# A head loop with memory features: five loads three steps later, and one constant on another engine

## Chip, cores and metric

The kernel runs on one core of a Trainium2 chip. The metric is the time of one execution on the device, in microseconds. Of the kernel before there are three timed runs: 708.89, 709.9 and 713.49 us, median 709.9. One execution was profiled; it took 710.93 us, and the span from its first to its last instruction is 709.2 us.

## What is computed

Two independent parts are computed and set side by side. Part B is a two-dimensional spectral filter (a real FFT over 2048 x 576, a product with learned weights, the inverse). Part A is attention with a compressive memory: 32 heads of width 18, and a sequence of 2048 rows in four segments of 512. In each segment a head attends within the segment, and also reads from a memory that was filled by the segments before. The change is in part A. The reference, cut to it:

```python
phi = lambda t: jnp.where(t > 0, t + 1.0, jnp.exp(t))
for s in range(N):                       # N = 4 segments of L = 512
    qs, ks, vs = q[:, :, s], k[:, :, s], v[:, :, s]
    p = _softmax(jnp.einsum("bhqd,bhkd->bhqk", qs, ks) * scale + mask, axis=-1)
    a_dot = jnp.einsum("bhqk,bhkd->bhqd", p, vs)
    pq = phi(qs)
    num = jnp.einsum("bhld,bhde->bhle", pq, M)
    den = jnp.einsum("bhld,bhd->bhl", pq, z)[..., None] + 1e-6
    o = g * (num / den) + (1.0 - g) * a_dot
    M = M + jnp.einsum("bhld,bhle->bhde", phi(ks), vs)
    z = z + jnp.einsum("bhld->bhd", phi(ks))
```

The features pq are phi(q). Segment 0 (the first) finds an empty memory and needs none; the second segment, g=1 in the code, is the first to read them. The 1e-6 is the small constant of the denominator's reciprocal.

## The kernel before

The kernel has three stages. In the first the forward FFT runs while part A's weights are split. In the second, the projections of part A are computed; queries, keys, values and the features go to DRAM, the queries and keys as three bf16 pieces each, whose sum has the precision of float32. The inverse FFT follows. The third stage is the attention; it holds the change.

**The head loop.** `attention` (L928) is a loop over t=0 to 132, one step per head and segment. Steps come in blocks of eight heads, a stack n = t//8; a segment is four stacks, 32 steps. Each step issues work of several pipeline depths at once:

- `s1` (L637) for head t+10: three score matmuls (L652 with L653, then two at L644) in PSUM banks of a tag with three buffers, and on VectorE the row maxima of them (L654, L648). It is the first work of a step.
- `s2` (L680) for head t: scores again (L688, L692, L693, L697), now transposed and with the maxima folded in; ScalarE takes the exponentials (L689, L694, L698). Every fourth step GpSimd then masks four blocks (L701).
- `pv` (L709): the product with the values, on alternate steps from t=5; `pv_out` (L721) copies the result to U, and `u_dmas` (L725) sends a stack's sums (rD, one transfer) and rows (uD, four) to DRAM.
- `mpath` (L662): every fourth step the maxima are split by GpSimd (L669, L670), turned by TensorE (L674) and written as two further rows of the query stack by a DMA that GpSimd issues (L678).

**The order of work** is written out by hand: each engine takes its instructions in program order, and SyncE issues nearly all DMAs in program order as well. At the first step of a stack (t%8 = 0) a list q is filled: six transfers of query stack n+2 (`stack_dmas`, tile Qs, three buffers), six of key stack n+3 (tile Ks; one of the four key buffers and one of the three query buffers are called x in the profile), and one `load_v` (tile vs). Each of the six moves 18 partitions of 8 heads, 144 KB. Two entries of the list are issued per step, so the queries go in steps t%8 = 0 to 2, the keys in 3 to 5, vs in 6. The sums and rows of an earlier stack (rD, uD) are interleaved with them in steps t%8 = 4 to 6. SyncE's DMAs use eight completion semaphores in turn; an issue waits until the DMA that used the same one before, eight issues earlier, has landed.

The query stack loaded in steps 16 to 18 (stack 4) takes the buffer of stack 1, which s2 reads until step 15. Because `s1` runs ten steps ahead, it is first read in step 22, by `s1` of head 32. The next one (stack 5) is loaded from step 24 on and first read in step 30.

**The features.** `pq_load` (L759, the DMA at L763) loads one of five tiles of features (126 partitions x 512 float32, the last 72 partitions) into one of five buffers. For the second segment it is called in the head loop, once a step, ahead of the step's entries of the list. In later segments `mem1` reloads a buffer when it has been read. The readers are `den` (L765), a generator put into the background list at t=34, whose matmuls (L772) form the denominators, and `mem1` (L788).

**The reciprocals.** `recip` (L736) is a generator that moves on once a step. It loads a 128 x 128 tile `ry` of denominators (L739), waits three steps, adds the constant if asked (L743), takes the reciprocal on VectorE (L744), scales it on ScalarE (L746), splits it into three bf16 pieces (L747 to L750, ScalarE and GpSimd) and sends these to DRAM. It runs eight times in all. Three of them, one for each of the segments 1 to 3, are called by `den` with the constant (`eps` true); the other five divide by the softmax sums and have none.

Of the kernel before, what the change touches and what calls it, by code (L numbers as in the profile page):

```python
# [389 lines left out]
class ATT:  # L390
# [345 lines left out]
    def recip(s,src,dst,gate,eps,load,slack=0):  # L736
        nc=s.nc; tp=s.tp
        w=tp.tile([128,3,128],BF,name="rw",bufs=2); y=tp.tile([128,128],F32,name="ry",bufs=2)
        nc.sync.dma_start(y,src.rearrange("h (b c) -> (h b) c",b=4))  # L739
        yield  # L740
        yield
        yield
        if eps: nc.vector.tensor_scalar(y,y,1e-6,None,op0=OP.add)  # L743
        nc.vector.reciprocal(y,y)  # L744
        yield
        nc.scalar.activation(y,y,AF.Copy,scale=gate)  # L746
        nc.scalar.copy(w[:,0],y)  # L747
        nc.gpsimd.tensor_tensor(y,y,w[:,0],op=OP.subtract)
        nc.gpsimd.tensor_copy(w[:,1],y)
        nc.gpsimd.tensor_tensor(w[:,2],y,w[:,1],op=OP.subtract)  # L750
        for _ in range(slack): yield
        nc.sync.dma_start(bass.AP(tensor=dst.tensor,offset=dst.offset,ap=[[128,128],[32*512,3],[1,128]]),w)
        yield
        yield
        r=tp.tile([96,512],BF,name=load,bufs=1) if load!="re" else tp.tile([126,1024],BF,name="re",tag="pq",bufs=5)[:96,:512]
        nc.sync.dma_start(r,dst)
        s.rc[load]=r
        yield
# [169 lines left out]
    def attention(s,tp,ps):  # L928
        nc=s.nc; s.tp,s.ps,s.psm,s.mtag=tp,ps,s.ps1,"s1"
        s.homes()  # L930
        def steps(gen,i):
            for _ in range(i):
                try: next(gen)
                except StopIteration: return
# [5 lines left out]
        def run_bg(rate):  # L940
            state["acc"]+=rate
            if state["acc"]>=1:
                state["acc"]-=1
                while bg:
                    try: next(bg[0]); break
                    except StopIteration: bg.pop(0)
        lane=[]
        s.cap=tp.tile([128,128],F32,name="cap",bufs=1)
        for t in range(133):
            k,hh=divmod(t,4); n,qd=divmod(k,2); g=k//8  # L950
            if t==3: nc.gpsimd.memset(s.cap,3.0e38)
            if t==4: nc.gpsimd.affine_select(out=s.cap,in_=s.cap,pattern=[[1,128]],compare_op=OP.is_ge,fill=0.0,base=0,channel_multiplier=-1)
            if hh==0 and qd==0:
                if 0<n<14: q+=s.stack_dmas(n+2,0)
                if 0<n<13: q+=s.stack_dmas(n+3,1)
                if n+2<16: q.append(lambda n=n: s.load_v(n+2))
            st=t%32
            if 16<=t<21: s.pq_load(1,t-16)
            if t==34: bg.append(s.den(1,lane))
            if st==8 and g>0:  # L960
                def ln(g=g):
                    r=s.recip(s.rD[g-1],s.rrD[g-1],s.g1,False,"rr",2)
                    for i in range(8):
                        next(r)
                        if 2<i<6: s.ux_load(g-1,i-3)
                        yield
                    yield from r
                    bg.append(s.mixed(g))
                    if g<3: bg.append(s.den(g+1,lane))
                    if g<3: bg.append(s.oproj(g-1))  # L970
                lane.append(ln())
            if t==124: lane.append(s.recip(s.rD[3],s.rrD[3],s.g1,False,"rr"))
            if 125<=t<128: s.ux_load(3,t-125)
            a=s.s1(t+10) if t+10<128 else iter(())
            b=s.s2(t) if t<128 else iter(())
            if q: q.pop(0)()
            if qu: qu.pop(0)()
            if hh==3 and m is not None: steps(m,1)
            steps(a,1)
            steps(b,1)  # L980
            r=(t-5)%4
            if r%2: run_bg(1)
            steps(a,1)
            steps(b,1)
            if 5<=t<129: s.pv((t-5)//4,(t-5)%4)
            if t==129:
                for j in range(4): s.pv(31,j)
                s.pv_out(31)
                u=s.u_dmas(15)
                rb=s.recip(s.rD[3],s.rrD[0],s.g1,False,"re")  # L990
                qu+=[u[0],lambda: next(rb)]+u[1:]
            steps(a,1)
            steps(b,1)
            if hh==2 and m is not None: steps(m,1)
            if hh==1 and k+2<32: m=s.mpath(k+2); next(m)
            if 7<=t<131 and t%4==3:
                s.pv_out((t-7)//4)
                if t%8==3:
                    u=s.u_dmas((t-11)//8)
                    if t<120: s.later(1,lambda u=u: qu.extend(u))  # L1000
                    else: qu+=u
            for l in list(lane):
                try: next(l)
                except StopIteration: lane.remove(l)
            if q: q.pop(0)()
            if qu: qu.pop(0)()
            run_bg((.3,1,.5,1)[r])
            s.due(t)
# [30 lines left out]
        nc=s.nc  # L1039
# [108 lines left out]
```

## Time and profile before

| What | Value |
|---|---|
| three timed runs | 708.89, 709.9, 713.49 us |
| median | 709.9 us |
| profiled execution | 710.93 us |
| its span | 709.2 us |
| TensorE matmul busy | 676.4 us (95%) |
| VectorE busy | 556.2 us (78%) |
| ScalarE busy | 441.0 us (62%) |
| GpSimd busy | 208.8 us (29%) |
| chain that ended last | TensorE 61%, VectorE 9%, DMA 6%, ScalarE 5% |
| moved by DMA | 121.04 MB, mean 171 GB/s |

In the profile PE is TensorE, PEld its weight loads, DVE VectorE, ACT ScalarE, POOL GpSimd and SPq SyncE's issue of DMAs. A row of the timeline has its start in us, its duration, engine, line of the kernel, operation, output<-inputs, and in brackets the idle time of the engine before it with what ended it. Releasers are inferred from semaphores, and several transfers share one, so the name in brackets can be that of a neighbour. A row of the table of windows has the stretch, its length, the busy time of each engine with its count of instructions, the granted share of TensorE's clock, the mean busy share of the core's 16 DMA engines, and GB/s. TensorE is busy in nearly all of the span; its idle places and its granted clock say where time can be won or lost.

### The profile page before, as it was taken

The page shows a single profiled execution, that of the slowest core. Times are in us where ns is not written, and L with a number is a line of the kernel's source. Part 1 is how long each engine was busy: PE and PEld are TensorE (multiplying, and loading weights), DVE is VectorE, ACT ScalarE, POOL GpSimd, SP SyncE. Part 2 cuts the span into 40 slices and gives each one's busy share as a digit, 9 for nine tenths or more (in the row PEclk, how much of TensorE's full clock was granted, in tenths as well). Part 3 has the DMA queues.
Part 4 walks back from the last instruction along what each step waited for, and adds up shares of the span by engine and source line. Part 5 has one row for each costly group of instructions (what it writes and reads, how often), then busy time and mean ns, then how long its engine had stood idle before and what let it go on. Part 6 is the DMA issues. An engine that isn't in the chain of part 4 may idle for free.

```text
span 709.2 us, 14168 instructions
## 1 busy us (share of the span) xinstructions
PE 676.4 (95%) x4861; PEld 498.7 (70%) x4861; DVE 556.2 (78%) x1233; ACT 441.0 (62%) x994; POOL 208.8 (29%) x409
## 2 busy tenths in 40 slices
PE   4999999999999999999999899999999999998997
PEld 4999779889879888999844444444566445764677
DVE  6999999899989889887588688877666876568153
ACT  3657695574574563444388677777666676567741
POOL 2110000100100111565165334555233753246210
PEclk9999999999999999999999999999999999999999
DMA  9876546555563568899647666676556765441331
GB/s 343 272 233 205 150 141 194 175 178 167 165 211 133 165 215 279 201 239 211 180 109 176 172 161 154 173 181 169 128 129 185 171 164 128 122 129 52 99 100 69
DMA packets 83388, 121.04 MB, mean 171 GB/s; under 512 B 11368, under 2 KB 50902, under 8 KB 83180
## 3 DMA queue, kind: packets, MB, share of 16 engines
q1 hardware_dynamic: 76724, 104.11, 51.8%
q0 software_dynamic: 6592, 16.03, 8.2%
q8 instruction: 38, 0.62, 0.4%
q14 instruction: 34, 0.28, 0.1%
HBM read 81.78 MB, written 38.24 MB: 169 GB/s over the span
## 4 chain that ended last, share of the span: by engine, by line
PE 61%; DVE 9%; DMA 6%; ACT 5%; issue 3%; POOL 3%; DVEq 0%; SPq 0%; ACTq 0%; POOLq 0%
PE pv L718 9%; PE po L861 7%; PE pj L464 6%; PE pjv L464 6%; PE s L644 5%; PE i L300 4%; PE i L311 4%; PE s L652 3%; PE s L688 3%; PE po L892 2%; DVE junk L648 2%; PE s L692 2%; PE pn L791 2%; PE pm L524 2%; PE s L653 2%
## 5 line engine op out<-in xcount | busy, mean ns | idle before, releaser
L648 DVE CUSTOM_DVE_ANT_0 junk<-s,mask 128x512 bf16<-128x512 f32 (+1 forms) x256 | 141.8, 554 | 55.1 <-PE s L644 44.3
L654 DVE TENSOR_REDUCE mx<-s 128x4 f32<-128x512 f32 x128 | 87.9, 687 | 20.0 <-PE s L653 18.2
L689 ACT ACTIVATE P<-s 128x512 f32<-128x512 f32 x128 | 77.2, 603 | 24.1 <-PE s L688 20.9
L718 PE MATMUL pv<-P,vs 128*32 128x512 f32 (+3 forms) x1024 | 82.3, 440 | 0.0
L694 ACT ACTIVATE P<-s 128x512 f32<-128x512 f32 x128 | 77.1, 602 | 6.9 <-PE s L693 3.8
L698 ACT ACTIVATE P<-s 128x256 f32<-128x256 f32 x128 | 49.6, 387 | 49.7 <-PE s L697 49.6
L701 POOL TENSOR_SCALAR_AFFINE_SELECT P<-P 128x512 f32<-128x512 f32 x116 | 69.4, 635 | 5.6 <-ACT P L689 4.7
L718 PEld LDWEIGHTS pv<-P,vs 128*32 128x32 f32 x1024 | 26.9, 109 | 45.0 <-issue 42.9
L464 PE MATMUL pj<-x,wqkh 128*128 128x512 f32 x162 | 56.1, 407 | 0.0
L210 DVE TENSOR_TENSOR t<-Z 128x580 f32<-128x580 f32 x64 | 46.7, 757 | 0.2
L514 POOL MEMSET vt<- 128x32 f32 x16 | 2.4, 159 | 148.8 <-PE pm L524 121.5
L210 DVE TENSOR_TENSOR Z<-t 128x580 f32<-128x580 f32 x64 | 45.9, 756 | 0.0
L644 PE MATMUL s<-Ks,Qs 108*128 108x512 bf16 (+1 forms) x128 | 42.2, 330 | 0.0
L488 ACT CAST sp<-pj 128x512 bf16<-128x512 f32 x36 | 21.1, 585 | 30.7 <-DVE pj L484 30.7
L142 PE MATMUL f<-ftab,eh 128*128 128x290 f32 (+1 forms) x160 | 31.6, 317 | 9.0 <-DMA ftab<-ftab 9.0
L300 PE MATMUL i<-civ,Y 128*128 128x256 f32 (+1 forms) x288 | 37.9, 284 | 1.6 <-DVE T L332 1.6
L300 PEld LDWEIGHTS i<-civ,Y 128*128 128x128 f32 (+1 forms) x288 | 35.8, 181 | 1.8 <-DVE T L332 1.8
L311 PE MATMUL i<-itab,T 128*128 128x290 f32 (+1 forms) x224 | 36.4, 312 | 0.0
L464 PEld LDWEIGHTS pj<-x,wqkh 128*128 128x128 f32 x162 | 30.4, 188 | 8.4 <-issue 1.7
L669 POOL CAST mh<-mg 128x16 bf16<-128x16 f32 x32 | 6.8, 214 | 99.1 <-ACT mg L667 67.9
L464 PE MATMUL pj<-xh,wqkh 128*128 128x512 f32 x90 | 35.6, 395 | 0.0
L464 PE MATMUL pj<-xh,wqkl 128*128 128x512 f32 x90 | 35.6, 395 | 0.0
(214 smaller groups left out, 1859.6 us busy)
## 6 DMA issues: line engine op xcount, KB each, us to landing
qkD<-sp SPq DMA_DIRECT2D x36, 384.0 KB
Ks<-qkD SPq DMA_DIRECT2D x72, 144.0 KB
x<-qkD SPq DMA_DIRECT2D x60, 144.0 KB
Qs<-qkD SPq DMA_DIRECT2D x60, 144.0 KB
xin<-xb SPq DMA_DIRECT2D x16, 384.0 KB
cfw<-cfw POOLq DMA_DIRECT2D x16, 384.0 KB, 4.5
civ<-civ POOLq DMA_DIRECT2D x16, 384.0 KB, 7.5
vs<-vD SPq DMA_DIRECT2D x16, 330.0 KB
```

Of the source, the lines that this page charges most:

```text
L210: v.tensor_tensor(o,a,b,op=op)
L300: nc.tensor.matmul(p[:m,k],Y[i][:,q,c*128:c*128+m],cc[:,hl,o:o+256],start=n==0,stop=n==5)
L311: nc.tensor.matmul(p,x,t,start=n==0,stop=n==6)
L464: s.nc.tensor.matmul(out,a,b,start=i==0,stop=i==len(L)-1)
L644: nc.tensor.matmul(out,Q[:108,h,128*i:128*i+128],K[:108,h,:128*(i+1)],start=True,stop=True)
L648: nc.vector.tensor_tensor_reduce(out=junk[:,:w],in0=src,in1=s.mask[:,512-w:],scale=1.0,scalar=-3.0e38, op0=OP.add,op1=OP.max,accum_out=s.m ...
L654: nc.vector.tensor_reduce(out=s.mx[k][:,hh],in_=pa.rearrange("p (b c) -> p b c",c=128),axis=mybir.AxisListType.X,op=OP.max)
L689: nc.scalar.activation(P[0][:,hh],p0,AF.Exp,scale=SC)
L694: nc.scalar.activation(P[1][:,hh],p1,AF.Exp,scale=SC)
L701: if k<29: nc.gpsimd.affine_select(out=x,in_=x,pattern=pat+[[1,128]],compare_op=OP.is_ge,fill=0.0,base=0,channel_multiplier=-1)
L718: nc.tensor.matmul(s.pvt[32*hh:32*hh+32,128*j:],vt[:,j,19*h:19*h+32],mv[0][:,hh,mv[1]],start=j==0,stop=j==2,skip_group_check=True)
L861: nc.tensor.matmul(ps,a[t][:r,c],b[:r,t,w],start=i==0,stop=i==14)
```

## The change

Two lines change. The five feature loads of the second segment are issued at t=19 to 23 instead of t=16 to 20; within the step the call stands where it stood, ahead of the step's list entries. The order on SyncE's queue was pq, two Qs, pq, two Qs, pq, two Qs, pq, two Ks, pq, Ks, rD, Ks, uD and so on; it becomes six Qs, pq, two Ks, pq, Ks, rD, Ks, uD, pq, Ks, uD, Ks, uD, pq, vs, uD, pq. And the addition of the constant in `recip` is issued on GpSimd; the reciprocal that follows stays on VectorE.

```diff
-        if eps: nc.vector.tensor_scalar(y,y,1e-6,None,op0=OP.add)
+        if eps: nc.gpsimd.tensor_scalar(y,y,1e-6,None,op0=OP.add)
...
-            if 16<=t<21: s.pq_load(1,t-16)
+            if 19<=t<24: s.pq_load(1,t-19)
```

## Prediction

> **What bounds the kernel now.** I read the page, then the chain of waits, then the waits and the timeline of TensorE around the moved loads (steps t=16 to t=32 of the head loop), then SyncE's own queue there, and last the table of windows for the clock and the DMA share. The chain is 61% TensorE, and in the attention part TensorE runs on almost without a break, so time is worth something only where it stops. In order, the rows below are one line of the chain and six of TensorE's timeline. The L697 matmul is the last of a step and L652 the first of the next.
>
> ```profile
> 390.54 6.15 DMA Ks<-qkD
> ```
> ```profile
> 390.63 0.27 PE L697 MATMUL s<-Qs,Ks 110*128 110x256 bf16 x1
> ...
> 394.50 0.28 PE L697 MATMUL s<-Qs,Ks 110*128 110x256 bf16 x1
> 396.82 0.38 PE L652 MATMUL s<-x,Qs 108*128 108x384 bf16 x2 [2.06 <-DMA Ks<-qkD]
> ...
> 402.11 0.28 PE L697 MATMUL s<-Qs,Ks 110*128 110x256 bf16 x1
> ...
> 413.77 0.28 PE L697 MATMUL s<-x,Ks 110*128 110x256 bf16 x1
> 413.88 0.38 PE L652 MATMUL s<-Ks,Qs 108*128 108x384 bf16 x2
> ```
>
> At step t=22 (s1(32), the first use of query stack 4) TensorE stands 2.06 us for a DMA: the only wait of TensorE for a transfer in the whole attention part. Two steps without a stop take 3.87 us (390.63 to 394.50); the two with it take 7.61 (394.50 to 402.11). So this place costs 3.74 us: 2.06 idle, and about 1.7 more. The other 1.7 is the granted clock in the table of windows (columns: PE, PEld, DVE, ACT, POOL busy, PEclk, DMA share, GB/s):
>
> ```profile
> 366.00:372.00 6.00, 6.00 (x51) 3.25 (x52) 5.18 (x16) 5.37 (x13) 4.14 (x7) 1.00 0.63 147
> ...
> 396.00:402.00 6.00, 5.17 (x34) 2.41 (x34) 3.12 (x8) 2.77 (x6) 1.98 (x4) 0.72 0.62 175
> ...
> 408.00:414.00 6.00, 6.00 (x57) 2.88 (x56) 5.04 (x16) 4.43 (x11) 3.00 (x5) 1.00 0.65 145
> ...
> 420.00:426.00 6.00, 6.00 (x47) 2.23 (x46) 4.10 (x14) 4.35 (x12) 0.42 (x2) 1.00 0.62 159
> ...
> 428.00:432.00 4.00, 4.00 (x37) 2.06 (x35) 3.51 (x13) 3.25 (x8) 1.28 (x3) 1.00 0.40 105
> ```
>
> In 396 to 402 the clock is 0.72: 6 x 0.28 = 1.7 us lost after the stop. The last-but-one column matters as much. Whatever is going on, the DMA share lies at 0.62 to 0.65 in these windows and falls to 0.40 only after 428. I read the flat 0.62 as the ceiling of these transfers: a stack transfer fills 18 partitions a piece and does not spread over all 16 engines, and the ones that it uses are never free.
>
> By the Trainium skill, "DMA: Bandwidth & Descriptors", section "Why a DMA increments its semaphore by 16 and not by 1", a SyncE transfer runs on the largest number of engines up to 16 that divides its slowest dimensions. Eighteen rows give nine engines, a share of 9/16 = 0.56. The plateau agrees, the other transfers making up the rest.
>
> SyncE's queue shows how the transfers stand in line:
>
> ```profile
> 381.98 0.32 SPq L763 DMA_DIRECT2D pq<-pqD  x1
> ...
> 386.65 0.32 SPq L763 DMA_DIRECT2D pq<-pqD  x1
> 387.02 1.25 SPq L628 DMA_DIRECT2D Qs<-qkD  x2
> 388.82 0.32 SPq L763 DMA_DIRECT2D pq<-pqD  x1
> 390.54 1.12 SPq L628 DMA_DIRECT2D Ks<-qkD  x2
> 392.53 0.30 SPq L763 DMA_DIRECT2D pq<-pqD  x1
> 393.43 0.27 SPq L628 DMA_DIRECT2D Ks<-qkD  x1
> 394.80 0.55 SPq L729 DMA_DIRECT2D rD<-U  x1
> 395.39 0.45 SPq L628 DMA_DIRECT2D Ks<-qkD  x1
> 396.54 0.27 SPq L734 DMA_DIRECT2D uD<-U  x1
> ...
> 402.56 3.73 SPq L628 DMA_DIRECT2D Qs<-qkD  x6
> 407.29 1.53 SPq L628 DMA_DIRECT2D Ks<-qkD  x3
> 411.11 0.54 SPq L729 DMA_DIRECT2D rD<-U  x1
> 411.70 0.46 SPq L628 DMA_DIRECT2D Ks<-qkD  x1
> 412.20 0.35 SPq L734 DMA_DIRECT2D uD<-U  x1
> 412.59 0.32 SPq L628 DMA_DIRECT2D Ks<-qkD  x1
> 413.43 0.27 SPq L734 DMA_DIRECT2D uD<-U  x1
> ```
>
> An issue takes over the semaphore of the one eight before it, and waits until that one has landed. So the eighth issue after a transfer tells when it was down. The sixth piece of query stack 4 (the second of the two at 387.02) has uD at 396.54 as its eighth: it landed at 396.5, and TensorE starts 0.28 later. The "Ks" that the wait row and the chain name is not wanted until t=30; the queries are what was missing. The sixth piece of stack 5 (end of the group at 402.56) has uD at 413.43 as its eighth. Its first use, L652 of t=30, begins at 413.88, right behind L697, with no idle. That is 0.45 us after the landing, of which 0.28 is the way from landing to start. Stack 5 comes 0.17 us before it would stop TensorE as well.
>
> **The loads, moved.** Five pq transfers (L763) go from t=16 to 20 to t=19 to 23, on SyncE's queue alone; nothing is added, and the issues (0.32 us each) are the same five. Between them they pass the six Qs pieces, the six Ks pieces, rD, the four uD and one vs. Three of them (381.98 to 386.65) stood in front of the last Qs piece, and no longer do.
>
> *At t=22.* Between the two landings (396.54 and 413.43, 16.89 us) lie twenty transfers: two pq, six Ks, six Qs, one rD, four uD, one vs. That is 0.84 us each. Three fewer in front bring stack 4 in 2.5 us earlier, at 394.0. By bytes it is more: 3 x 126 x 512 x 4 bytes at the 175 GB/s of the window is 4.4 us, which gives 392.1. TensorE is ready at 394.78 (end of L697). Both ends are early enough, so the stop goes: -3.74 us, clock included.
>
> *At t=30.* This is what is late next. Stack 5 cannot overtake: ahead of it in the line, before and after the change, stand the same five pq, six Qs, six Ks, rD, four uD and vs. The order among them is all that differs. If the engines that carry them were never free before, the last piece of stack 5 lands at 413.43 again. TensorE however comes 3.74 us earlier, at 413.88 - 3.74 = 410.14. It then waits until 413.43 + 0.28 = 413.71: +3.57 us. Bounds: 0, if there were gaps to fill; +3.57 if there were none. I take +3.57, as the plateau shows no gap and eight transfers are always open.
>
> *The clock after it.* The stop of 2.06 us cost 1.7 behind it; a stop of 1.58 elsewhere cost nothing:
>
> ```profile
> 282.15 2.04 PE L300 MATMUL i<-civ,Y 128*128 128x256 f32 x15 [1.58 <-DVE T L332]
> ```
> ```profile
> 282.00:284.00 2.00, 1.85 (x15) 1.85 (x16) 0.53 (x2) 0.12 (x1) 1.06 (x3) 1.00 0.93 197
> ```
>
> So the bounds for a stop of 3.57 are 0 and +1.7, and the nearer row is that of 2.06: I take +1.7. Before, those 1.7 us lay ahead of t=30 and were covered, because the queries of t=30 would not have been there sooner. Now they come behind t=30, where nothing waits, and are paid in full. The stage from t=32 on has room: the DMA share falls to 0.40 in it.
>
> By the Trainium skill, "TensorE: Matmul & The Clock Gate", section "Why this matters for your kernels", idle gaps over about 3 us between matmuls bring the half clock. The trace differs: 2.06 us was enough here. By that rule a stop of 3.57 still pays the 1.7, and the sum stays; were the stop under 3, it would be 0 and the sum +1.4 - 1.7 = -0.3, the second rival below.
>
> *Who reads pq.* The first reader is den(1):
>
> ```profile
> L772 PE MATMUL pd<-pq,zst x30: 592/605/617, 422.3 to 593.6; 126*32 126x512 f32 x24, 72*32 72x512 f32 x6
> ```
>
> It starts at 422.3. All pq are in line before stack 5, so down by 413.4: 8.9 us of cover. Nothing.
>
> **The constant on GpSimd.** Three times L743 leaves VectorE (0.22 us) and becomes a GpSimd instruction on which VectorE's reciprocal, next in VectorE's order, waits. Below are the group of the nearest GpSimd operation on this tile and rows of the three places.
>
> ```profile
> L748 POOL TENSOR_TENSOR ry<-ry,rw x8: 426/427/431, 446.1 to 683.1; 128x128 f32<-128x128 f32 x8
> ```
> ```profile
> 440.94 0.22 POOL L670 TENSOR_TENSOR mh<-mg,mh 128x16 bf16<-128x16 f32 x1
> 442.26 0.22 DVE L743 TENSOR_SCALAR ry<-ry 128x128 f32<-128x128 f32 x1
> 446.65 0.38 PE L652 MATMUL s<-Ks,x 108*128 108x384 bf16 x2 [0.93 <-DVE mx L654]
> ```
> ```profile
> 525.98 0.95 DVE L744 RECIPROCAL ry<-ry 128x128 f32<-128x128 f32 x1
> 526.28 0.22 POOL L670 TENSOR_TENSOR mh<-mg,mh 128x16 bf16<-128x16 f32 x1
> ```
> ```profile
> 616.34 0.22 POOL L670 TENSOR_TENSOR mh<-mg,mh 128x16 bf16<-128x16 f32 x1
> 619.74 0.22 DVE L743 TENSOR_SCALAR ry<-ry 128x128 f32<-128x128 f32 x1
> ```
>
> Its duration is bounded by 0.22 (the VectorE row) and 0.43 (L748, two inputs, same shape); I take 0.35 as one input on GpSimd lies between. In the first place GpSimd is free from 441.16, done by 441.6, and VectorE saves 0.25 at 442.26; VectorE is what TensorE waits for there (0.93 at 446.65), so up to -0.25. In the third GpSimd is free from 616.56, three microseconds ahead: VectorE saves 0.25, TensorE does not wait for it: 0. In the second GpSimd comes to it only after L670, at 526.5; the reciprocal starts at about 527.0 instead of 525.98. That is 1.0 us of VectorE, of which TensorE sees what three score banks do not absorb: between 0 and +1.0. The next score into that bank is due at 528.6 and its reduction would end about then, so I take +0.15. What GpSimd does next (a query DMA, then masks) waits for other engines in every place and starts no later. Sum: -0.1, bounds -0.5 and +1.0.
>
> **Sum.** -3.74 + 3.57 + 1.7 - 0.1 = +1.4 us. The profiled execution took 710.93 us (span 709.2), 1.0 over the median of 709.9, which itself has 708.89 to 713.49 around it. On the profiled one it gives 712.3; on the median 711.3, which I predict. About 1% (7.1 us) is what a measurement of this kernel can tell from no change.
>
> **The rivals.**
> First, the stop goes and does not come back. This needs free engine time between 382 and 413, about 3.6 us of it in 31. A share of 0.62 speaks for it if it is read as room; the steady plateau, the eight open transfers and the landing only 0.17 us ahead of t=30 speak against it. -3.74 - 0.1: 706.1.
> Second, the stop moves to t=30 but the clock stays up, or drops where TensorE has slack: -3.74 + 3.57 - 0.1 = -0.3, so 709.6. The 1.58 us stop speaks for it, the 2.06 us one against. This is also the case in which the change does nothing.
> Third, slower: the stop at t=30 brings two half-clock stretches. One place, one mechanism: if a stop of about 2.06 fills enough of one clock interval, one of 4.12 can spoil two. It decides from an idle of 4.12 on, thus if stack 5 lands 0.55 us later than I have it. Price +0.55 + 1.7 over the sum: +3.65, 713.6.
>
> **How the numbers follow.** Chances: my forecast 0.55, the second rival 0.2, the first 0.15, the third or a worse second place on GpSimd 0.10. The forecast's own range is 710.4 to 712.9, from the bounds of the constant (+1.1, -0.4) and half a microsecond either way for the two landings. With the second rival this holds 0.75, so the range reaches to the first too: 706.0 to 713.2. All cases lie within 1% of 709.9 (702.8 to 717.0): within 1% 0.94, faster by over 1% 0.02, slower by over 1% 0.04 for what a second late stack would add.
>
> **What would show it.** Right: no wait of TensorE at t=22; one of 3 to 4 us on L652 at t=30, with six Qs pieces landing at about the same time after t=16 as before; clock 1.00 around t=23 and a dip in the 6 us behind t=30; TensorE waiting for no DMA after that. The reciprocal of the second place starts some 0.5 us behind L670. Wrong: no wait at t=30 (then the engines had room); a share well over 0.65 in the stretch; or VectorE standing more than a microsecond for GpSimd in any place.

## Result and profile after

| What | Before | Changed |
|---|---|---|
| median | 710.6 us (20 runs, 707.47 to 713.49) | 715.08 us (20 runs, 711.32 to 718.65) |
| ratio of the times | | 1.0069, 95% interval 1.0053 to 1.0085 |
| profiled execution (span) | 710.93 us (709.2) | 711.75 us (710.0) |
| mean granted clock of the runs | 0.9979 to 0.9986 (three groups of runs beside the experiments) | 0.9957 |

The change costs 4.5 us. That is within 1%, as forecast, but 3.8 us above the forecast number, and above the upper end of the range. The profiled execution of the changed kernel is one of its fastest (711.75 against a median of 715.08), so its trace shows only a small part of the loss. This governs the whole reading below.

TensorE around the moved loads, and the starts of steps t=14, 38, 70 and 78, in the changed kernel's timeline:

```profile
379.36 0.38 PE L652 MATMUL s<-Ks,x 108*128 108x384 bf16 x2
...
395.47 0.28 PE L697 MATMUL s<-Qs,Ks 110*128 110x256 bf16 x1
395.58 0.38 PE L652 MATMUL s<-x,Qs 108*128 108x384 bf16 x2
...
411.08 0.27 PE L697 MATMUL s<-x,Ks 110*128 110x256 bf16 x1
413.06 0.39 PE L652 MATMUL s<-Ks,Qs 108*128 108x384 bf16 x2 [1.71 <-DMA Qs<-qkD]
...
430.69 0.38 PE L652 MATMUL s<-Ks,x 108*128 108x384 bf16 x2
...
467.62 0.38 PE L652 MATMUL s<-x,Qs 108*128 108x384 bf16 x2 [1.42 <-DMA Ks<-qkD]
...
512.08 0.38 PE L652 MATMUL s<-Ks,Qs 108*128 108x384 bf16 x2
...
538.84 0.38 PE L652 MATMUL s<-Ks,Qs 108*128 108x384 bf16 x2
```

At t=22 (395.58) L652 follows L697 directly: the stop is gone. At t=30 (413.06) TensorE waits 1.71 us for the queries. A second stop of 1.42 us stands at t=54 (467.62), the first use of the third segment's first query stack. Its table of windows, for the stretches of before:

```profile
396.00:402.00 6.00, 6.00 (x53) 3.01 (x55) 5.35 (x19) 5.11 (x14) 3.42 (x7) 1.00 0.76 197
...
408.00:414.00 6.00, 4.29 (x37) 1.98 (x35) 3.65 (x12) 3.30 (x9) 1.34 (x4) 1.00 0.64 167
414.00:420.00 6.00, 6.00 (x54) 3.14 (x56) 5.37 (x17) 5.08 (x13) 3.00 (x5) 1.00 0.71 200
420.00:426.00 6.00, 6.00 (x53) 2.20 (x45) 4.11 (x12) 4.35 (x11) 0.99 (x3) 1.00 0.62 160
```

In this execution the clock column stays at 1.00 behind the stop. The last column but one reaches 0.76 and 0.71, so the 0.62 of before was no ceiling. The trace of before shows that as well, in windows that the prediction left out:

```profile
384.00:390.00 6.00, 5.78 (x54) 2.81 (x57) 5.47 (x18) 4.93 (x13) 1.81 (x6) 1.00 0.82 195
...
402.00:408.00 6.00, 6.00 (x54) 3.28 (x51) 5.18 (x16) 4.75 (x12) 1.53 (x4) 1.00 0.71 165
...
414.00:420.00 6.00, 6.00 (x51) 3.16 (x49) 5.36 (x17) 5.03 (x13) 3.41 (x7) 1.00 0.74 179
...
432.00:436.00 4.00, 3.63 (x33) 1.64 (x31) 3.16 (x11) 2.77 (x8) 2.12 (x5) 1.00 0.88 189
```

The second place of the reciprocals, with all engines:

```profile
525.92 0.22 POOL L670 TENSOR_TENSOR mh<-mg,mh 128x16 bf16<-128x16 f32 x1
526.23 0.53 POOL L743 TENSOR_SCALAR ry<-ry 128x128 f32<-128x128 f32 x1
526.79 0.95 DVE L744 RECIPROCAL ry<-ry 128x128 f32<-128x128 f32 x1 [1.34 <-POOL ry L743]
...
527.66 0.63 DVE L654 TENSOR_REDUCE mx<-s 128x4 f32<-128x512 f32 x1
...
528.34 0.22 PE L674 MATMUL mt<-idb,mh 128*128 128x128 bf16 x1 [1.05 <-DVE mx L654]
```

GpSimd adds the constant behind its own L670, in 0.53 us. VectorE stands 1.34 us in front of the reciprocal, which starts 1.2 us later after the start of t=70 than before (526.79 - 512.08 = 14.7 us against 525.98 - 512.43 = 13.6). The maxima L654 come behind it on VectorE, and TensorE stands 1.05 us at L674, the transpose of the maxima.

### The profile page after: what moved, and what is told of

The parts are those of the page before. It is cut to its first block, busy times and chain, and to the rows that moved or that the text cites. A ratio compares the mean times of both kernels' runs of the same rounds, so it can differ in the third digit from the quotient of the medians.

```text
span 710.0 us, 14168 instructions
## 1 busy us (share of the span) xinstructions
PE 674.8 (95%) x4861; PEld 497.3 (70%) x4861; DVE 555.3 (78%) x1230; ACT 441.2 (62%) x994; POOL 211.0 (30%) x412
## 3 DMA queue, kind: packets, MB, share of 16 engines
q1 hardware_dynamic: 76724, 104.11, 51.8%
## 4 chain that ended last, share of the span: by engine, by line
PE 58%; DMA 11%; DVE 7%; ACT 6%; issue 2%; POOL 2%; SPq 1%; DVEq 0%; ACTq 0%; POOLq 0%
PE pv L718 9%; PE pjv L464 8%; PE pj L464 7%; PE po L861 7%; PE s L644 4%; DMA yb<-yout 4%; DMA x<-qkD 3%; PE s L652 3%; PE i L300 3%; PE s L688 3%; PE po L892 2%; PE i L311 2%; PE s L692 2%; PE pn L791 2%; PE pm L524 2%
## 5 line engine op out<-in xcount | busy, mean ns | idle before, releaser
L654 DVE TENSOR_REDUCE mx<-s 128x4 f32<-128x512 f32 x128 | 87.9, 686 | 20.6 <-PE s L653 18.8
L718 PEld LDWEIGHTS pv<-P,vs 128*32 128x32 f32 x1024 | 26.8, 109 | 44.6 <-issue 42.2
```

Of the source, the lines that this page charges most:

```text
L654: nc.vector.tensor_reduce(out=s.mx[k][:,hh],in_=pa.rearrange("p (b c) -> p b c",c=128),axis=mybir.AxisListType.X,op=OP.max)
L718: nc.tensor.matmul(s.pvt[32*hh:32*hh+32,128*j:],vt[:,j,19*h:19*h+32],mv[0][:,hh,mv[1]],start=j==0,stop=j==2,skip_group_check=True)
```

## The same stretches in all traces

I cut the span at the first L652 of six steps, t=14, 38, 46, 54, 70 and 78. From t=78 to the end all traces agree within 0.3 us (171.1 to 171.4). Ahead of t=14 they do not: it starts at 377.5 to 380.4 us, and at 378.39 and 379.69 in the two traces of before. In the changed kernel neither of the two lines acts there, so spans of single traces do not tell two kernels apart to within 3 us. From the rows above, t=14 to 38 of the changed kernel is 430.69 - 379.36 = 51.3 us, and 70 to 78 is 538.84 - 512.08 = 26.8. The others are worked out in the same way.

| Kernel traced | 14 to 38 | 38 to 46 | 46 to 54 | 54 to 70 | 70 to 78 |
|---|---|---|---|---|---|
| before | 53.1 | 17.7 | 18.8 | 44.4 | 25.6 |
| before, once more (control) | 52.0 | 17.7 | 19.2 | 44.6 | 25.6 |
| changed | 51.3 | 17.4 | 19.5 | 44.5 | 26.8 |
| changed, once more (after_again) | 54.4 | 17.4 | 19.5 | 44.5 | 26.8 |
| loads_only | 52.1 | 17.7 | 18.0 | 45.0 | 25.6 |
| eps_only | 50.6 | 17.4 | 19.2 | 46.7 | 26.8 |
| eps_sooner | 51.6 | 17.4 | 18.9 | 44.5 | 25.6 |
| after_sooner | 50.0 | 17.4 | 19.7 | 44.8 | 25.6 |
| bridge | 51.2 | 17.7 | 18.5 | 44.9 | 25.6 |
| pq_late | 51.5 | 17.7 | 20.4 | 44.9 | 25.6 |
| double | 55.0 | 17.7 | 18.4 | 45.4 | 25.6 |
| pq_early | 49.5 | 17.7 | 18.3 | 44.6 | 25.6 |
| early_eps | 49.5 | 17.4 | 18.1 | 44.4 | 26.8 |
| early_sooner | 49.5 | 17.4 | 18.2 | 44.7 | 25.6 |

The columns 38 to 46 and 70 to 78 hold the first and the second place of the reciprocals and depend on the constant alone. The column 14 to 38 holds the loads; it varies by up to 3 us between two executions of one kernel (51.3 and 54.4). The 46.7 of eps_only in 54 to 70 holds a wait of 2.4 us for a feature tile reloaded in a later segment, at that length in no other trace (1.14 in double, 0.6 at most elsewhere).

## Experiments

My theory (A in the expectations) keeps the prediction's mechanism: the loads only move the stop along a line of transfers that is nearly full, and the constant costs what its second place shows. The rivals put the loss into the loads alone, into the constant alone, or into transfer time left unused at t=16; each expectation says what they give. All ratios are to the kernel before on the same chip, with 95% intervals.

### The two parts alone

loads_only keeps the constant on VectorE; eps_only keeps the loads at t=16 to 20.

```diff
loads_only
-            if 16<=t<21: s.pq_load(1,t-16)
+            if 19<=t<24: s.pq_load(1,t-19)
eps_only
-        if eps: nc.vector.tensor_scalar(y,y,1e-6,None,op0=OP.add)
+        if eps: nc.gpsimd.tensor_scalar(y,y,1e-6,None,op0=OP.add)
```

> Only the five feature loads move to t=19 to 23; the constant stays on VectorE. Theory A (saturated DMA line): TensorE does not stop at t=22, stops 1.5 to 3.6 us at t=30, and in many executions pays a half-clock stretch of 1.7 us behind it; time +1 to +4 us against the kernel before, most of the measured +4.5. Theory B (the GpSimd addition is the cost): the loads are worth nothing or a gain, 0 to -2 us, and the whole slowdown is missing here.

Measured: 711.99 us against 710.68, ratio 1.0020 (0.9995 to 1.0045). TensorE waits 2.51 us at t=30 in its timeline, with no half clock behind:

```profile
412.12 0.27 PE L697 MATMUL s<-x,Ks 110*128 110x256 bf16 x1
414.90 0.34 PE L652 MATMUL s<-Ks,Qs 108*128 108x384 bf16 x1 [2.51 <-DMA Qs<-qkD]
```

> Only the addition of the constant goes to GpSimd; the loads stay at t=16 to 20. Theory A: +1 us, the 1.1 us by which the reciprocal of the second place came later in the changed kernel's profile, the two other places free; TensorE stops at t=22 as before. Theory B: +3.5 to +4.5 us, that is nearly all of the slowdown.

Measured: 711.53 us against 710.68, ratio 1.0028 (1.0009 to 1.0047), that is +2.0 us by the ratio and +0.9 by the medians. The trace shows where +0.9 comes from: 38 to 46 is 0.3 shorter than before (17.4 against 17.7), 70 to 78 is 1.2 longer (26.8 against 25.6). Its mean clock equals that of before beside it (0.9986 both). Against the expectation TensorE does not stop at t=22 in this trace; it waits 0.79 us at t=30.

What follows: the constant costs something, and neither part costs the whole 4.5 us. The interval of the loads reaches down to no cost. The constant, forecast at -0.1, costs about +0.9 in the trace.

### The loads elsewhere

pq_early issues the five loads at t=0 to 4, pq_late at t=27 to 31. The constant stays on VectorE in both.

```diff
pq_early
-            if 16<=t<21: s.pq_load(1,t-16)
+            if t<5: s.pq_load(1,t)
pq_late
-            if 16<=t<21: s.pq_load(1,t-16)
+            if 27<=t<32: s.pq_load(1,t-27)
```

> The loads are issued at t=0 to 4, where the DMA engines of the kernel before had free time (nothing moved from 360 to 362 us), the constant stays on VectorE. Theory A: some 4 us of work leave the saturated stretch, TensorE stops neither at t=22 nor at t=30, no half-clock stretch in between: -2 to -4 us. Rival (the stop is not one of engine time but of the order in the queue alone): t=22 is free as with the move to t=19, and t=30 stops all the same; 0 to +3 us.

Measured: 708.15 us against 710.68, ratio 0.9977 (0.9951 to 1.0003). No stop is left at t=22, 30 or 54, and 14 to 38 falls to 49.5 us.

> The loads are issued at t=27 to 31, behind the queries of stack 5 too; the first reader is still the denominators after t=34. Theory A: stacks 4 and 5 both come in time, so no stop at t=22 and t=30; the loads use the room from 428 us on, but stack 6 (t=32 to 34, first read at t=38, 3.7 us of room before) or the denominators may now be late by 0 to 2 us: -3 to 0 us in all. Rival (order alone): the stop goes on to t=38 in full, 0 to +3 us.

Measured: 713.56 us, ratio 1.0057 (1.0029 to 1.0085). This is a miss of theory A. The long stops at t=22 and 30 did go (14 to 38 is 51.5, with small stops in it), but later ones came; these are rows from its waits of TensorE in the attention part (total us, times, longest):

```profile
PE s L652 <- DMA Qs<-qkD: 1.2, 1, 1.2
PE pb L824 <- DMA rr<-rrD: 0.9, 1, 0.9
PE pd L772 <- DMA pq<-pqD: 0.9, 2, 0.6
```

46 to 54 takes 20.4 us, the longest of all: L824 waits for the reciprocals `rr`, and L652 at t=54 for the queries (the control, with no change, has 1.17 there). Of the 0.9 us for features (L772) only 0.24 stand at the den of the second segment, at 420.85 us; its last matmuls stand 0.66 more, which the view puts down to ScalarE. The other 0.6 is a later segment's, at 502 us, and loads_only has 0.61 there too. The expectation had named the denominators, and not L824. Where the rest of the 2.9 us lies is not shown.

### How full the line is

double adds work to the kernel before: beside each of the five loads another one of the same 252 KB, into buffers that nothing reads for the output.

```diff
-            if 16<=t<21: s.pq_load(1,t-16)
+            if 16<=t<21:
+                s.pq_load(1,t-16)
+                x=s.tp.tile([126,512],F32,name="am",bufs=5); nc.sync.dma_start(x,s.pqD[1][0:126])
```

> The kernel before with five more feature loads of the same size (252 KB each, into buffers that are not read before they are overwritten) beside the five at t=16 to 20. Theory A (the DMA line is saturated): five more transfers at 0.84 to 1.0 us each make t=14 to t=38 longer by 4 to 5 us (54.5 to 58 us), and the time rises by 3 to 6 us with the half clock. Rival (a share of 0.62 is room): less than 1 us.

Measured: 717.16 us against 711.47 (4 runs), ratio 1.0118 (1.0059 to 1.0177). That is +5.7 us by the medians and +8.4 by the ratio. The stop at t=22 grows to 3.1 us, and the clock dips behind it. The den that waits for features is a later segment's, at 504 us, and not the reader of the five loads. Rows of its waits of TensorE, then of its windows:

```profile
PE s L652 <- DMA pq<-pqD: 3.1, 1, 3.1
...
PE pd L772 <- DMA pq<-pqD: 1.1, 1, 1.1
```
```profile
396.00:402.00 6.00, 3.59 (x21) 1.92 (x25) 2.85 (x7) 2.22 (x6) 1.25 (x4) 0.82 0.71 178
```

Five loads fewer give 49.5 us for 14 to 38, five more 55.0, against 53.1 and 52.0 in the two traces of before. The line is full enough that added transfers are paid by TensorE. It is not so full that each is paid in whole: five times 252 KB at the 178 GB/s of that window would be 7.2 us (an estimate), and the stretch grew by 1.9 to 3.0.

### Transfer time left unused at t=16

In the changed kernel SyncE's first feature load came behind the six query pieces. SyncE's queue, and the windows of 2 us of the changed kernel and then of the control:

```profile
383.77 2.90 SPq L628 DMA_DIRECT2D Qs<-qkD  x6
386.71 0.34 SPq L763 DMA_DIRECT2D pq<-pqD  x1
```
```profile
384.00:386.00 2.00, 1.75 (x12) 0.89 (x11) 1.79 (x9) 1.96 (x6) 1.70 (x3) 1.00 0.60 162
386.00:388.00 2.00, 2.00 (x23) 0.88 (x22) 1.75 (x6) 1.05 (x3) 0.00 (x0) 1.00 0.62 144
```
```profile
384.00:386.00 2.00, 1.75 (x14) 1.05 (x13) 1.93 (x7) 1.89 (x5) 2.00 (x4) 1.00 1.02 225
386.00:388.00 2.00, 2.00 (x22) 0.73 (x20) 1.81 (x7) 1.33 (x3) 0.05 (x1) 1.00 0.79 211
```

Before the change the engines carry features together with the queries (1.02 and 0.79; the view books a packet's whole time where it starts, so a short window can pass 1). After it the share is only 0.60 and 0.62. bridge puts one load back to t=16, constant on VectorE.

```diff
-            if 16<=t<21: s.pq_load(1,t-16)
+            if t==16 or 20<=t<24: s.pq_load(1,max(t-19,0))
```

> The first feature load stays at t=16, ahead of the queries, the other four go to t=20 to 23; the constant stays on VectorE. Theory A3 (the load at t=16 is a bridge: it waits for nothing, so it keeps the DMA engines fed while SyncE waits for the query buffer; moved away, the engines run dry for 1 to 2 us): the concurrency of DMA packets does not fall below 10 around the first query of stack 4, t=30 is reached about 1 us earlier than with all five moved, and the time is that of the kernel before, -1 to +0.5 us. Rival (the move costs because more loads stand right ahead of stack 5): as the loads alone, +1 to +2 us.

Measured: 711.71 us against 711.23, ratio 1.0010 (0.9984 to 1.0037), stop at t=30 1.58 us. It cannot be told from loads_only (1.0020). Its share in 384 to 388 was 0.62 and 0.63, but it is 1.1 us ahead of the changed kernel there (t=14 at 378.30 against 379.36); in 382 to 384, with its one load, it was 1.01, where the changed kernel has 0.98. The experiment is inconclusive.

### The place of the constant on GpSimd

eps_sooner issues the addition one yield, thus one step, ahead of the reciprocal; the loads stay at t=16 to 20. early_eps has the loads at t=0 to 4 with the constant as in the change.

```diff
eps_sooner
         yield
         yield
+        if eps: nc.gpsimd.tensor_scalar(y,y,1e-6,None,op0=OP.add)
         yield
-        if eps: nc.vector.tensor_scalar(y,y,1e-6,None,op0=OP.add)
         nc.vector.reciprocal(y,y)
```

> Loads at t=16 to 20; the constant on GpSimd, but issued one step sooner than the reciprocal that needs it. Theory A (the cost of the constant is VectorE standing at the second place until GpSimd has come to it): no wait of VectorE for GpSimd there, and VectorE has three times 0.22 us less: 0 to -0.5 us. Rival (GpSimd's addition costs by itself, by holding up GpSimd's masks or sharing memory with VectorE): +1 to +2 us as with the constant alone.

Measured: 711.22 us against 711.23, ratio 1.0000 (0.9976 to 1.0025). 70 to 78 is back at 25.6, and the 0.3 of the first place stays won (17.4). The addition takes as long as in the changed kernel; the line's group shows all three, and nobody waits for them. At the second place the reciprocal and L674 run without a wait; the group, then the two rows:

```profile
L742 POOL TENSOR_SCALAR ry<-ry x3: 528/533/547, 440.6 to 615.9; 128x128 f32<-128x128 f32 x3
```
```profile
525.02 0.94 DVE L744 RECIPROCAL ry<-ry 128x128 f32<-128x128 f32 x1
...
526.78 0.22 PE L674 MATMUL mt<-idb,mh 128*128 128x128 bf16 x1
```

> The loads at t=0 to 4 and the constant on GpSimd. If the constant costs the 1.05 us wait at the second reciprocal and no more, this is 0.8 to 1.1 us over the early loads alone (-2.5), so -1.4 to -1.7 us against the kernel before. If the constant makes other stops worse, it is +2 us over them, so about -0.5 us.

Measured: 709.75 us, ratio 0.9973 (0.9951 to 0.9995). 70 to 78 is 26.8 again: the wait at the second place has nothing to do with where the loads are. That the constant costs 0.8 to 1.1 us over the early loads alone is not seen in the times: pq_early has 0.9977, on another chip.

### The changed kernel and the kernel before, once more

> The changed kernel once more, beside the other parts on one chip. Theory A1 (the two parts add): the sum of the parts measured alone, +1.4 and +0.9 to +2, so +2.3 to +3.4 us. Theory A2 (they make each other worse, through more half-clock stretches): +4 to +6 us again, with a mean granted clock below that of either part alone (0.9977 and 0.9986).

Measured: 715.34 us against 711.23, ratio 1.0057 (1.0028 to 1.0085); mean clock 0.9962 against 0.9979. The +4.1 us by the ratio is what A2 gives, but its interval (+2.0 to +6.0) holds A1 as well. This trace shows what the first of the changed kernel did not: 3.04 us of stop and the half clock behind it. Its timeline, then its windows:

```profile
410.17 0.27 PE L697 MATMUL s<-x,Ks 110*128 110x256 bf16 x1
413.48 0.61 PE L652 MATMUL s<-Ks,Qs 108*128 108x384 bf16 x2 [3.04 <-DMA Qs<-qkD]
```
```profile
408.00:414.00 6.00, 2.96 (x28) 1.19 (x26) 2.40 (x10) 2.20 (x6) 0.43 (x3) 0.96 0.64 166
414.00:420.00 6.00, 6.00 (x42) 3.06 (x41) 4.09 (x11) 3.55 (x9) 2.77 (x5) 0.76 0.67 194
```

The clock loses 6 x 0.04 + 6 x 0.24 = 1.7 us.

> The kernel before, one more look, to see how far the stop at t=22 of its first profile (2.06 us, with 1.7 us of half clock) is typical. If it is, t=14 to t=38 take 53 us again; if it was one of several patterns, t=14 to t=38 take 50.5 to 52 us, with the stop at t=30 or shared, and without half clock.

Measured (one run): 711.73 us, span 710.0. The kernel before stops for 1.37 us at t=22 and for 0.84 at t=30, without half clock. Its timeline and its window there:

```profile
397.45 0.38 PE L652 MATMUL s<-x,Qs 108*128 108x384 bf16 x2 [1.37 <-DVE mg L666]
...
414.03 0.39 PE L652 MATMUL s<-Ks,Qs 108*128 108x384 bf16 x2 [0.84 <-DMA Qs<-qkD]
```
```profile
396.00:402.00 6.00, 4.63 (x41) 2.52 (x41) 3.98 (x14) 3.36 (x10) 2.44 (x6) 1.00 0.64 146
```

So the half clock on which the prediction rested belonged to that execution of before, not to every one.

### Both parts with the constant one step sooner

after_sooner has the loads at t=19 to 23, early_sooner at t=0 to 4; both have the edit of eps_sooner.

> Loads at t=19 to 23 as in the changed kernel, but the constant on GpSimd one step sooner than its reciprocal. If the wait of VectorE at the second place is all that the constant adds, this is the loads alone: +1 to +2 us. If the constant on GpSimd makes the stops of the moved loads worse in some other way, it stays at +4 us.

Measured: 712.45 us against 711.47, ratio 1.0019 (0.9991 to 1.0048). Beside the changed kernel's 1.0057 to 1.0069 this is some 3 us better, for one line moved ahead of a yield; after_again and after_sooner ran on different chips, each against the kernel before beside it.

> Loads at t=0 to 4 and the constant on GpSimd one step sooner: both costs taken out. Theory A: -2 to -3 us against the kernel before, at or a little under the early loads alone (-1.6 to -2.5). Rival (the early loads gain only by luck of the runs): within 0.5 us of the kernel before.

Measured: 708.82 us against 711.47 (12 runs, 705.78 to 710.54), ratio 0.9973 (0.9948 to 0.9998): the lowest ratio, with early_eps, and an interval that ends just below 1. Against the kernel before it wins 1.9 us by the ratio. Its windows show where the loads went:

```profile
354.00:360.00 6.00, 5.20 (x35) 2.62 (x36) 5.57 (x19) 5.34 (x13) 4.73 (x10) 1.00 0.93 282
360.00:366.00 6.00, 5.87 (x58) 2.86 (x51) 4.90 (x17) 4.36 (x12) 3.86 (x7) 1.00 0.37 84
...
408.00:414.00 6.00, 6.00 (x58) 2.93 (x59) 5.16 (x17) 4.28 (x12) 2.52 (x6) 1.00 0.81 158
```

The loads fall into 354 to 360 (0.93). At 360 to 366, behind them, the DMA engines still have room (0.37), and at 408 to 414 TensorE is busy throughout.

## Why the prediction was right and wrong

The time came out 3.8 us above the forecast. Over the runs the moved loads alone cost about what their three terms add up to, so the error lies mainly in the term of the constant: forecast -0.1, by the ratios +2.0 alone and some +3 beside the moved loads, of which the traces show 0.9. The sections follow the prediction's order.

**The stop at t=22 goes.** Right: no wait there in any trace with the loads at t=19 to 23. The credit was mis-sized. The 2.06 us were real; the 1.7 us of half clock behind them were there in one traced execution only. The control has 1.37 without it, eps_sooner 2.02 without it, and eps_only no stop there. Across the four traces with the five loads alone at t=16 to 20 (53.1, 52.0, 50.6, 51.6), t=14 to 38 takes 51.8 us on average. With the loads moved (51.3, 54.4, 52.1, 50.0) it takes 52.0. So the loads neither win nor lose much in the traced executions, as -3.74 + 3.57 without the +1.7 behind it had it. Over the runs they cost 1.4 us where the constant stays on VectorE (loads_only, 1.0020) and where it is issued a step sooner (after_sooner, 1.0019), both intervals reaching to no cost. That is close to the +1.5 of -3.74 + 3.57 + 1.7. That agreement is luck: the traces show none of the three terms at its size as a rule.

**The stop at t=30 comes back.** Right in kind: 1.71, 3.04 and 2.51 us, on L652, for the queries. One trace, after_sooner, has only 0.35. 3.57 was the upper bound and too high; the control shows that before also stops there (0.84). The step that failed is "the plateau shows no gap". The share was not flat: in the trace of before it is 0.82, 0.71 and 0.74 between the windows that were read, in the control 1.02, and in early_sooner 0.81 without the five loads. So 0.62 was the share of one mix of transfers, and as a mean over 16 engines it does not tell whether the engines of a stack transfer were free. pq_early and double do show the weaker form: fewer transfers in the stretch end the stop, more of them lengthen it.

**The clock behind t=30.** Right in after_again (1.7 us), absent in the first trace and in loads_only. It is a matter of how often, which one trace cannot tell: of the four traces of the paragraph on t=22 with the loads at t=16 to 20 one has a half-clock stretch, and of the four with the loads moved one. The mean clock of the runs tells more. On the same chip it fell from 0.9979 to 0.9962, worth 0.0017 x 710 = 1.2 us. The forecast had set credit and debit equal. Run by run, the mean clock was below 0.998 in 27 of the 90 runs of before beside the experiments, and in 25 of the 32 of the changed kernel. But the runs at 0.998 or above took 710.0 us on average before (63 runs) and 713.4 changed (7 runs), so by these few runs most of the loss is not half clock. Where the further stretches lie in the executions that were not traced is not shown.

Stops of 2.06, 3.04 and 3.13 us were followed by half clock, those of 2.02 and 2.51 were not: no fixed length decides. By the Trainium skill, "TensorE: Matmul & The Clock Gate", section "What's actually happening", the clock is judged in windows of 3413 ns that run freely, so that the point of change varies with where in a window the work falls. The traces agree: each of the three half-clock stretches lasted 3.41 us (in before the clock reads 0.50 from about 397.7 to 401.1 us), and the same kernel has it in one execution and lacks it in the next.

**The readers of pq.** Right: no wait of den in the changed kernel. pq_late, eight steps later again, is the case where that cover is gone (0.24 us of waiting at its den).

**The constant.** Wrong. Forecast -0.1, measured about +0.9 in the traces: -0.3 at the first place, +1.2 at the second. Two things in that step failed. The duration is 0.53 us and not 0.35: the group of L748, two inputs, 0.43, was no upper bound for one input. That cost little, as the reciprocal comes 1.2 us late against the 1.0 forecast. The step that failed is "what three score banks do not absorb", which was read for the score matmuls alone. In this part of the loop (k of 10 and more) `mpath` takes the bank of its transpose `mt` from the same three-buffer tag as the scores, the `else` branch of its choice of pool. The transpose therefore waits for the late maxima L654, and 1.05 us of the delay reaches TensorE at L674. The prediction had named the sign to look for, VectorE standing more than a microsecond for GpSimd, and its upper bound (+1.0 at that place) was nearly right; the value taken (+0.15) was not. That the cost hangs on the addition standing right ahead of the reciprocal is shown by eps_sooner: a step sooner the wait is gone and the ratio falls from 1.0028 to 1.0000 (the intervals, 1.0009 to 1.0047 and 0.9976 to 1.0025, overlap). That the 1.2 us at the second place are all of it is not shown: by the ratios the constant costs 2.0 us alone, some 3 beside the moved loads (the changed kernel against after_sooner), and nothing beside the early ones (early_eps and early_sooner, both 0.9973).

**No DMA wait after that.** Wrong: TensorE waits 1.42 us at t=54 (1.46 in after_again). The control waits 1.17 there and the first trace of before 0.67, so little of it is the change's. The room that the prediction saw from t=32 on, a share of 0.40, was one window of 4 us; the next one, 432 to 436, has 0.88.

**What stays open.** By the ratios the parts cost 1.4 and 2.0 us, the whole 4.0 to 4.9. The difference of 0.6 to 1.5 us lies within the intervals of up to 2 us on each. The stretches of the two traces of the changed kernel cover only a part of the loss: against the mean of before and control they are 0.3 us longer in 14 to 38, 0.5 in 46 to 54 and 0.9 at the two places of the constant. Where the difference is real, the lower clock of the whole (0.9957 and 0.9962, against 0.9977 for loads_only and 0.9986 for eps_only) covers about 0.0018 x 710 = 1.3 us of it. Why the two parts together should fall into the half clock more often than the loads alone is not settled.

## What to carry to other kernels

A transfer moved later in a line that is nearly full can move the stop along with it; look instead at every window of the trace, not at a choice of them, for a stretch where the engines idle, as t=0 to 4 here. When an operation goes to another engine whose result the next instruction wants at once, issue it a step ahead, and list every user of the buffers behind the waiting instruction, not only the obvious one. One profiled execution can hold a half-clock stretch that most do not: price such a term from several traces, or from the mean clock of the runs.

## What was new about the hardware

GpSimd took 0.527 to 0.547 us for a constant added to a 128 x 128 float32 tile, more than the 0.43 us of its own subtraction of two tiles of that size, and more than twice VectorE's 0.22. By the Trainium skill, "GPSIMD Engine Reference", section "4.1 Engine selection", element-wise work belongs on VectorE, but with one input GpSimd runs at roughly line rate. The advice agrees with these rows; the remark on one input does not, at 0.53 us against 0.22.
